# A gated mix of linear attention and a gMLP: token-major spatial product, one fused GELU ahead of all Exp, attention from unnormalised exponentials, DMA transposes

## The chip, the cores and the metric

The kernel runs on one core of one Trainium2 chip. The metric is device time in microseconds (us). Engines are named as in the profile: PE is the matrix engine (PEld its weight loads), DVE the vector engine, ACT the scalar (activation) engine, POOL the general engine, SP the engine whose queue issues most DMAs. A profiled span is some 2 us shorter than a timed run. Every ratio below is the mean time of one kernel's fast runs over the mean of the old kernel's fast runs of the same rounds on the same chip, with a 95% interval, so it is not quite the ratio of the medians that stand beside it.

## The reference

2048 tokens of width 512 go through two branches, which a sigmoid gate mixes. Branch A is linear attention with 32 heads of 16: the features are softmax(pq) and softmax(-pq). Branch B is a gMLP: GELU of an input product, half of it layer-normalised and multiplied over the token axis by a 2048x2048 matrix (the "spatial product"), times the other half, then an output product.

```python
pq = einsum('bhsd,hdf->bhsf', q, w_phi); pk = einsum('bhsd,hdf->bhsf', k, w_phi)
phi_q = concat([softmax(pq), softmax(-pq)]); phi_k = concat([softmax(pk), softmax(-pk)])
kv = einsum('bhsf,bhsd->bhfd', phi_k, v); z = einsum('bhsf->bhf', phi_k)
a = (phi_q @ kv / (phi_q @ z + 1e-06)) @ wo
zz = gelu(x @ w_in)                      # tanh form, 1376 features
z1, z2 = zz[..., :688], layernorm(zz[..., 688:])
b = (z1 * (w_sp @ z2 + b_sp[:, None])) @ w_out
out = g * a + (1 - g) * b                # g = sigmoid(x . gate_w)
```

## The kernel before

A first loop over 16 token tiles makes z2, the gate logit, K and V. GELU is built from five passes; Tanh and Exp are in use alternately (the trace has a single table load). `...` marks cuts.

```python
for tt in range(NT):
    ... # matmuls: z2_ps (128x689), v_ps, pk_ps
    nc.scalar.activation(out=xc[:, :], in_=z2_ps[:, 0:FH], func=AF.Copy)
    nc.vector.tensor_tensor(out=sq[:], in0=xc[:], in1=xc[:], op=ALU.mult)
    nc.vector.scalar_tensor_tensor(out=arg[:], in0=sq[:], scalar=INV_K, in1=xc[:], op0=ALU.add, op1=ALU.mult)
    nc.scalar.activation(out=th[:], in_=arg[:], func=AF.Tanh, scale=CK)
    nc.vector.scalar_tensor_tensor(out=z2all[:, tt, :], in0=th[:], scalar=1.0, in1=xc[:],
        op0=ALU.add, op1=ALU.mult, accum_out=s_z2[:, tt:tt + 1])
    nc.scalar.activation(out=junk[:], in_=z2all[:, tt, :], func=AF.Square, accum_out=s_sq[:, tt:tt + 1])
    ... # ek = exp(+-pk) on ACT; zk (reduce), rk (reciprocal), phik = ek * rk on DVE
```

The second half works feature-major in chunks of 512 tokens. z2 is the stationary operand of the spatial product (`lhsT` in the code; the other operand, `rhs`, is passed through it column by column, and these are the moving columns), so 688 features take six tiles of 128, the last with 48 useful rows but the full cost in moving columns. Attention normalises through PE: a block mask product sums the exponentials, and further products make denominators and spread their reciprocals.

```python
def gg_chunk(c, z1p, ft_list, uT, wspT):
    for ft in ft_list:                     # 6 feature tiles, the last 48 wide
        for st in range(NT):
            nc.tensor.matmul(gg_ps[0:m, :], lhsT=z2all[:, st, ft * P:ft * P + m], rhs=wspT[:, st, :], ...)
        ... # + bias row, * z1 (two DVE passes of 128x512)
def q_pre(c):
    for g in range(NDT):
        ... # e1, e2 = exp(+-pq)
        nc.tensor.matmul(s2p[:, :], lhsT=mask_bd[:, :], rhs=e2[:, :], ...)   # sums, spread
        nc.vector.tensor_tensor(out=phi1[:, :], in0=e1[:, :], in1=s2p[:, :], op=ALU.mult)
        ... # the same for phi2
    ... # den_ps: 8 products
def o_chunk(c, phi, rden):
    for g in range(NDT):
        nc.tensor.matmul(rbp[:, :], lhsT=selp[:, g, :], rhs=rden[:, :], ...)  # spread 1/den
        ... # nump: 2 products; ot = nump * rb
```

The softmax here doesn't subtract the row's maximum and nothing guards it: scores larger than these inputs give would overflow.

## Time and profile before

| | before |
|---|---|
| time, median (range) | 281.97 us (280.68 to 283.1) |
| profiled span | 279.6 us |
| PE, DVE, ACT busy | 246.8, 216.2, 148.4 us |
| moving columns on PE, counted in the source | about 548,500 |

The head of the page gives busy time per engine, and the span in 40 slices of 7 us, each digit a busy share in tenths (9 is 90% or more).

```profile
span 279.6 us, 3333 instructions
...
PE 246.8 (88%) x1213; PEld 112.6 (40%) x1236; DVE 216.2 (77%) x398; ACT 148.4 (53%) x263; POOL 6.7 (2%) x23
...
PE   0668799999888369999999999999999999999993
...
DVE  0067999999999999999989954589965489955442
```

DVE is at its top from the fifth slice to the twentieth, PE from the sixteenth to the last but one; before that PE falls to 3 tenths in one slice. The table of stages makes it firm. Its columns are the stretch and its length in us, busy us (and instructions) of PE, PEld, DVE, ACT and POOL, the share of its full clock that PE was granted, the DMA share and GB/s.

```profile
14.00:106.00 92.00, 75.27 (x434) 37.43 (x442) 86.62 (x176) 69.03 (x132) 0.00 (x0) 0.94 0.41 91
...
124.00:270.00 146.00, 145.06 (x644) 62.82 (x655) 109.34 (x175) 58.21 (x100) 0.00 (x0) 1.00 0.16 40
60.00:90.00 30.00, 26.88 (x148) 12.95 (x148) 30.00 (x56) 26.09 (x50) 0.00 (x0) 1.00 0.00 1
```

In the first loop (14 to 106 us) PE is idle for 92.00 - 75.27 = 16.7 us and DVE is 94% busy, from 60 to 90 us without a gap; in the second (124 to 270) PE has 145.06 of 146. So two different limits follow each other, with a stretch between (106 to 140 us, not shown) in which both engines are nearly full. The chain of waits says the same:

```profile
PE 57%; DVE 29%; ACT 4%; SPq 4%; DMA 3%; issue 2%; ACTq 0%
```

The passes of the built-up GELU in the list of groups (busy us, then mean ns of one, then idle time before them):

```profile
L214 DVE SCALAR_TENSOR_TENSOR z2all<-th,xc 128x688 bf16<-128x688 bf16 x16 | 14.0, 873 | 0.5 <-ACT th L213 0.5
L211 DVE SCALAR_TENSOR_TENSOR arg<-sq,xc 128x688 bf16<-128x688 bf16 x16 | 14.0, 873 | 0.1
...
L213 ACT ACTIVATE th<-arg 128x688 bf16<-128x688 bf16 x16 | 12.5, 780 | 7.6 <-DVE arg L211 7.4
L206 ACT ACTIVATE xc<-z_ps 128x688 bf16<-128x688 f32 x16 | 11.8, 735 | 15.6 <-PE z_ps L202 15.6
...
L209 DVE TENSOR_TENSOR sq<-xc 128x688 bf16<-128x688 bf16 x16 | 7.9, 495 | 0.0
```

### The profile page before, as it was taken

What the parts mean: (1) busy time and instruction counts of PE and PEld (TensorE: products, weight loads), DVE (VectorE), ACT (ScalarE), POOL (GpSimd) and SP (SyncE); (2) the same over time, 40 slices, a digit from 0 to 9 for tenths busy, and PEclk for the clock granted to TensorE, in tenths of its full rate; (3) what the DMA queues carried; (4) which work ended last, traced back from release to release, by engine and by line L of the source; (5) the groups of instructions that cost most, each with busy time, mean ns of one, the idle gap of its engine ahead of it and who ended that gap; (6) DMA issues with size and microseconds to landing.
All of it is one profiled execution on the core that took longest, in us unless ns stands there. A gap on an engine that the chain in (4) does not pass through costs nothing.

```text
span 279.6 us, 3333 instructions
## 1 busy us (share of the span) xinstructions
PE 246.8 (88%) x1213; PEld 112.6 (40%) x1236; DVE 216.2 (77%) x398; ACT 148.4 (53%) x263; POOL 6.7 (2%) x23
## 2 busy tenths in 40 slices
PE   0668799999888369999999999999999999999993
PEld 0234444444443137334434444444444444444441
DVE  0067999999999999999989954589965489955442
ACT  1154777897898649772448512158622156332033
POOL 9000000000000000000000000000000000000000
PEclk9998999999999879999999999999999999999999
DMA  6999997000000000000019110076010000010001
GB/s 167 218 233 232 221 263 248 4 0 0 0 2 0 0 0 4 0 0 2 1 28 272 40 38 0 1 175 146 19 38 0 2 0 0 19 60 0 0 19 56
DMA packets 51727, 17.53 MB, mean 63 GB/s; under 512 B 46800, under 2 KB 51584, under 8 KB 51712
## 3 DMA queue, kind: packets, MB, share of 16 engines
q1 hardware_dynamic: 51568, 16.81, 25.8%
q0 software_dynamic: 144, 0.52, 0.7%
q8 instruction: 9, 0.15, 0.2%
q14 instruction: 6, 0.05, 0.1%
HBM read 3.70 MB, written 2.10 MB: 21 GB/s over the span
## 4 chain that ended last, share of the span: by engine, by line
PE 57%; DVE 29%; ACT 4%; SPq 4%; DMA 3%; issue 2%; ACTq 0%
PE gg_ps L416 29%; PE z_ps L371 6%; PE b_ps L434 6%; DVE zk L228 5%; DVE phik_st L242 4%; PE a_ps L440 4%; DVE z2all L214 4%; DVE arg L211 3%; DMA wqkT<-in_A_wqkv_dram 3%; DVE phik_lv L236 3%; DVE rk L233 3%; PE den_ps L358 3%; SPq L114 2%; PE rbp L399 2%; DVE sq L209 1%
## 5 line engine op out<-in xcount | busy, mean ns | idle before, releaser
L416 PEld LDWEIGHTS <-z2all 128*128 128x128 bf16 (+1 forms) x384 | 37.4, 98 | 48.1 <-issue 5.2
L416 PE MATMUL gg_ps<-wsp_87,z2all 128*128 128x512 bf16 (+1 forms) x188 | 45.4, 379 | 0.2
L416 PE MATMUL gg_ps<-wsp_88,z2all 128*128 128x512 bf16 (+1 forms) x188 | 44.5, 379 | 0.2
L201 PE MATMUL z_ps<-w_in_g,xT 128*128 128x512 bf16 x62 | 22.7, 403 | 11.6 <-DMA w_in_g<-in_B_w_in_dram 9.1
L421 DVE TENSOR_TENSOR ggb<-gg_ps,brow 128x512 f32<-128x512 f32 (+1 forms) x24 | 16.4, 687 | 19.7 <-PE gg_ps L416 19.1
L401 ACT ACTIVATE rb<-rbp 128x512 bf16<-128x512 f32 x16 | 9.6, 597 | 40.6 <-PE rbp L399 40.6
L371 PE MATMUL z_ps<-xT,w_in_g 128*128 128x512 bf16 (+1 forms) x92 | 25.0, 398 | 1.5 <-DVE stat L207 1.1
L203 PE MATMUL v_ps<-wv_sb,xT 128*128 128x512 bf16 x61 | 20.6, 406 | 2.9 <-ACT vz_all L220 2.7
L206 ACT ACTIVATE xc<-z_ps 128x688 bf16<-128x688 f32 x16 | 11.8, 735 | 15.6 <-PE z_ps L202 15.6
L204 PE MATMUL pk_ps<-wk_p,xT 128*128 128x512 bf16 x63 | 17.7, 378 | 2.5 <-ACT ek L226 2.0
L228 DVE TENSOR_REDUCE zk<-ek 128x64 f32<-128x1024 bf16 x16 | 19.4, 1213 | 0.2 <-ACT ek L226 0.2
L260 PE MATMUL pq_ps<-xT,wq_p 128*128 128x512 bf16 x63 | 16.8, 379 | 0.4 <-ACT pqT_all L264 0.4
L452 ACT ACTIVATE ot_bf<-tmp,stat 128x512 bf16<-128x512 f32 x16 | 11.4, 720 | 10.3 <-DVE tmp L447 8.8
L213 ACT ACTIVATE th<-arg 128x688 bf16<-128x688 bf16 x16 | 12.5, 780 | 7.6 <-DVE arg L211 7.4
L202 PE MATMUL z_ps<-w_in_g,xT 128*128 128x177 bf16 x64 | 16.2, 254 | 0.1
L219 ACT ACTIVATE junk<-z2all 128x688 bf16<-128x688 bf16 x16 | 12.5, 780 | 6.6 <-DVE z2all L214 6.6
L447 DVE SCALAR_TENSOR_TENSOR tmp<-a_ps,stat,b_sb 128x512 f32<-128x512 f32 x16 | 11.3, 727 | 5.6 <-ACT b_sb L445 5.6
L445 ACT ACTIVATE b_sb<-b_ps 128x512 f32<-128x512 f32 x16 | 9.5, 591 | 10.7 <-PE b_ps L434 10.5
L371 PEld LDWEIGHTS <-w_in_g 128*128 128x128 bf16 (+1 forms) x96 | 9.4, 102 | 13.7 <-issue 5.3
L392 DVE RECIPROCAL rden<-den_ps 128x128 bf16<-128x128 f32 x16 | 14.5, 930 | 0.7 <-PE den_ps L358 0.7
L214 DVE SCALAR_TENSOR_TENSOR z2all<-th,xc 128x688 bf16<-128x688 bf16 x16 | 14.0, 873 | 0.5 <-ACT th L213 0.5
L211 DVE SCALAR_TENSOR_TENSOR arg<-sq,xc 128x688 bf16<-128x688 bf16 x16 | 14.0, 873 | 0.1
(486 smaller groups left out, 447.9 us busy)
## 6 DMA issues: line engine op xcount, KB each, us to landing
out_dram<-ot_bf SPq DMA_DIRECT2D x16, 128.0 KB, 1.7
w_in_g<-in_B_w_in_dram SPq DMA_DIRECT2D x2, 688.0 KB, 6.0
w_out_t<-in_B_w_out_dram SPq DMA_DIRECT2D x1, 640.0 KB, 6.4
brow<-in_B_b_sp_dram POOLq DMA_DIRECT2D x1, 512.0 KB, 5.6
wv_sb<-in_A_wqkv_dram SPq DMA_DIRECT2D x1, 512.0 KB, 7.6
wo_t<-in_A_wo_dram SPq DMA_DIRECT2D x1, 512.0 KB, 6.9
xT<-in_A_x_dram SPq DMA_TRANSPOSE x5, 4.9
w_out_t<-in_B_w_out_dram SPq DMA_DIRECT2D x1, 48.0 KB, 6.1
```

The lines of the kernel that those rows point to most:

```text
L201: nc.tensor.matmul(z2_ps[:, 0:CH], lhsT=lhsT, rhs=w_in_g[:, dt, FH:FH + CH], start=st_, stop=sp_)
L202: nc.tensor.matmul(z2_ps[:, CH:FH + 1], lhsT=lhsT, rhs=w_in_g[:, dt, FH + CH:F + 1], start=st_, stop=sp_)
L203: nc.tensor.matmul(v_ps[:, :], lhsT=lhsT, rhs=wv_sb[:, dt, :], start=st_, stop=sp_)
L204: nc.tensor.matmul(pk_ps[:, :], lhsT=lhsT, rhs=wk_p[:, dt, :], start=st_, stop=sp_)
L211: nc.vector.scalar_tensor_tensor(out=arg[:], in0=sq[:], scalar=INV_K, in1=xc[:], op0=ALU.add, op1=ALU.mult)
L214: nc.vector.scalar_tensor_tensor(out=z2all[:, tt, :], in0=th[:], scalar=1.0, in1=xc[:], op0=ALU.add, op1=ALU.mult, accum_out=s_z2[:, tt:tt ...
L228: nc.vector.tensor_reduce(out=zk[:, :], in_=ek[:].rearrange("p a (h e) -> p (a h) e", e=DH), axis=AX.X, op=ALU.add,)
L260: nc.tensor.matmul(pq_ps[:, :], lhsT=wq_p[:, dt, g * P:(g + 1) * P], rhs=xT[:, dt, c0:c0 + CH], start=(dt == 0), stop=(dt == NDT - 1),)
L371: nc.tensor.matmul(z1_ps[0:m, :], lhsT=w_in_g[:, dt, jt * P:jt * P + m], rhs=xT[:, dt, t0:t0 + CH], start=(dt == 0), stop=(dt == NDT - 1),)
L416: nc.tensor.matmul(gg_ps[0:m, :], lhsT=z2all[:, st, ft * P:ft * P + m], rhs=wspT[:, st, :], start=(st == 0), stop=(st == NT - 1),)
L421: nc.vector.tensor_tensor(out=ggb[0:m, :], in0=gg_ps[0:m, :], in1=brow[0:m, t0:t0 + CH], op=ALU.add)
L434: nc.tensor.matmul(b_ps[:, :], lhsT=uT[ft][:, t4 * P:(t4 + 1) * P], rhs=w_out_t[:, ft, :], start=(ft == 0), stop=(ft == NFT - 1),)
```

## The change

The intent is fewer PE columns and far less DVE work. (1) z2 becomes the moving operand of the spatial product (344 of 688 features at a time, no padding; the output has tokens on partitions, so the bias is a per-partition scalar and one DVE pass replaces two). (2) One fused GELU activation replaces the five passes, and the whole GELU stage is written ahead of everything with Exp, because the two need different ACT tables. (3) For queries the raw exponentials are multiplied by [kv | z | block mask] in one 144-column product; sums and denominators come out as columns, and the division is done on the 512 outputs per token. (4) What is now token-major (attention output, gated features) is brought to the output products by DMA transposes. (5) `w_sp` is loaded whole. The core of the diff, cut:

```diff
-        nc.scalar.activation(out=xc[:, :], in_=z2_ps[:, 0:FH], func=AF.Copy)
-        ... sq, arg, th, z2all (as above)
+    def z2_tile(tt):
+        zp = z_mm(tt, FH, FH + 1)
+        nc.scalar.activation(out=z2v, in_=zp[:, :, 0:HF], func=AF.Gelu_apprx_tanh)
+        ... # bn_stats, bn_aggr for the layer norm
+    for c in range(NCH):                   # all of z2 and z1 before the first Exp
+        for tt in ts: z2_tile(tt)
+        for tt in ts: z1_tile(tt)
+        z2_norm(ts)
 ...
+    def attn_tile(tt):
+        for a in range(2):
+            for g in range(NG):
+                nc.tensor.matmul(at[:, a, g, 0:AW], lhsT=eq[a][:, g, t0:t0 + P], rhs=kvz[:, a * 4 + g, :], ...)
+        ... # sd, t12, den, rden, r (small), m = at * r, o = m0 + m1
+        nc.sync.dma_start_transpose(out=oT[:, :, :], in_=o[:, :])
+    def gg_half(tt, j):
+        for st in range(NT):
+            nc.tensor.matmul(gp[:, :], lhsT=wspT[:, st, tt * P:(tt + 1) * P],
+                             rhs=z2all[:, st, j * HF:(j + 1) * HF], ...)
+        nc.vector.scalar_tensor_tensor(out=ucat[tt % NU][:, j * HF:(j + 1) * HF], in0=gp[:, :],
+            scalar=bT[:, tt:tt + 1], in1=z1all[:, tt, j * HF:(j + 1) * HF], op0=ALU.add, op1=ALU.mult)
+    def u_T(tt):
+        nc.sync.dma_start_transpose(out=uT[:, :, :], in_=ucat[tt % NU][:, :])
+    for tt in range(NT):
+        gg_half(tt, 0)
+        if tt >= 1: oTs[tt - 1] = attn_tile(tt - 1)
+        gg_half(tt, 1)
+        uTs[tt] = u_T(tt)
+        if tt >= 2: ba_tile(tt - 2, ...)   # 4 + 6 output products, one scaled copy, store
```

## The prediction

> **What bounds the kernel now.** The page shows a span of 279.6 us with PE busy 246.8 (88%), DVE 216.2 (77%), ACT 148.4 (53%). The table of stages shows three parts. To 9 us PE waits for input weights (one 9.1 us wait in the list of waits). From about 14 to 106 us DVE sets the pace: the tanh-GELU built from DVE and ACT passes (sq 495 ns, arg 873, z2all 873), zk 1213, rk 556, phik 556+827; in 60 to 90 us DVE is busy 30.0 of 30, PE 26.9. From 124 us to the end PE is full at clock 1.00 (29.9 of 30). The chain of waits agrees: PE 57%, DVE 29%.
>
> **Cost of PE work.** In the trace a 128x512 matmul starts every 215 ns, a 128x129 one every 57 ns, weight loads hidden: the N/2.4 + 2.5 ns of the Trainium skill, "TensorE: Matmul & The Clock Gate", section "Back-to-back issue gap". Counting moving columns from both sources: before 548,500 (229 us at full rate), after 484,000 (202 us; about 206 with the fixed cost). Saved: the padded sixth feature tile of spatial product and z1, and the ones-mask, denominator and broadcast products, partly offset by 144-column attention products.
>
> **What DVE and ACT lose.** One GELU activation replaces copy, sq, arg, tanh and the final product. From the 735 ns copy of 128x688 I estimate 0.74 us; "ScalarE: Activation LUTs" of the Trainium skill, section "Step-by-step: what each stage is for", says throughput does not depend on the function; no run here shows it yet. DVE estimates scaled from traced passes: bn_stats 0.45 us each, normalise 0.45.
>
> **Stage by stage (estimates).**
> - Start: first matmul at 8.5 us (w_in now split over ACT's queue).
> - GELU stage: 88,000 columns, 37.5 us on PE; ACT about 24 plus extra table loads (the order shows the gate's Exp placed between GELUs; 1.3 us each), DVE about 23. PE-bound with a cold clock at first: ends at 48.
> - Weight folding: eight 0.69 us casts in a row, partly covered by v and k products: 6 us, to 54.
> - K/V/Q stage: per tile PE 3.05, ACT 5 x 0.6 = 3.0, DVE 1.21+0.56+1.3 = 3.1 us, balanced; 50 us, to 104; draining the last tiles' DVE chain adds 3: 107.
> - Spatial/attention/output stage: per tile PE (32x344 + 8x144 + 10x512 columns) 7.3 us, DVE about 3.7; 117.6 us. The transposed attention output is needed about 7 us after its DVE chain allows issue, and two transposes are issued in order on SP. With the input transposes' 4.7 to 4.9 us landing and 1.3 us issue the margin is under 1 us, so I allow 5 us of PE stalls: 230.
> - Tail: DVE chain of the last tile, transpose, ten matmuls, store: 9 us, span about 239; times run about 2 us over the span.
>
> Predicted 240 us, 80% range 228 to 262. Chances: faster by over 2% 0.91, within 2% 0.03, slower 0.06.
>
> **What would show each step.** PE busy about 212 and over 88% of the span; DVE near 150, ACT near 100; gp matmuls every 146 ns; no stage with DVE above 90% except perhaps K/V/Q; PE waits on oT small; inputs (14 MB) landed by about 65 us.
>
> **What would make it wrong.** SBUF-to-SBUF transposes costing far more than input ones (issue of several us each): every output tile would wait, adding 16 times the excess. Next: the K/V/Q stage, where three balanced engines may wait for each other (+5 to 10 us); start-up DMA order; Pool's pow or DVE broadcast reads from PSUM slower than estimated.

## The result

The new kernel takes 237.0 us (236.57 to 238.69, 4 runs) against 281.33 us (280.3 to 283.1): ratio 0.8432, interval 0.8381 to 0.8482. The profiled span fell from 279.6 to 235.2 us. The page of the new kernel, the same lines as before (slices are now 5.9 us):

```profile
span 235.2 us, 3568 instructions
...
PE 212.9 (91%) x1412; PEld 127.9 (54%) x1412; DVE 149.0 (63%) x335; ACT 82.1 (35%) x133; POOL 9.9 (4%) x38
...
PE   0289999969999999995999999999999999999953
...
DVE  0035747677999999997177745577455775556750
```

PE busy fell by 33.9 us and PE's idle time by 10.5 us (from 32.8 to 22.3); together that is the 44.4 us of the span. The chain of waits is now

```profile
PE 62%; DVE 28%; DMA 6%; issue 2%; ACT 1%; SPq 1%; POOLq 0%; DVEq 0%; POOL 0%; ACTq 0%
```

Most of DVE's share in it is the K chain of the K/V/Q stage (phik 8%, zk 7%, rk 4%); e9 asks whether that chain sets the pace.

I cut the stages where the trace shows the last matmul of the GELU stage (54.5 us), the first K sum on DVE (60.15), and the first and last spatial matmul (109.4, 221.3):

```profile
12.87:54.50 41.63, 39.71 (x254) 25.20 (x254) 25.75 (x86) 25.64 (x35) 5.07 (x8) 1.00 1.19 236
54.50:60.15 5.65, 5.54 (x49) 3.40 (x49) 5.19 (x10) 4.02 (x6) 0.00 (x0) 1.00 1.30 284
60.15:109.40 49.25, 46.02 (x305) 24.66 (x304) 47.07 (x57) 40.13 (x77) 0.00 (x0) 1.00 0.08 25
109.40:221.30 111.90, 111.89 (x762) 70.90 (x763) 65.66 (x175) 8.94 (x13) 0.00 (x0) 0.98 0.28 59
221.30:235.20 13.90, 7.69 (x40) 3.09 (x37) 5.29 (x12) 2.06 (x3) 0.00 (x0) 1.00 0.25 61
```

The spatial stage has PE busy 111.89 of 111.90 us, so PE has no gap there; e3 tests whether its columns set the time. The groups that answer to those of before, and the spatial product:

```profile
L371 PE MATMUL gp<-z2all,wspT 128*128 128x344 bf16 x512 | 81.1, 313 | 0.8 <-DVE kvz L319 0.8
...
L184 DVE BATCH_NORM_STATS2 bn_83<-z2all 128x6 f32<-128x344 bf16 x32 | 14.9, 501 | 0.0
L181 ACT ACTIVATE z2all<-zp 128x688 bf16<-128x688 f32 x16 | 11.9, 744 | 15.2 <-PE zp L172 15.2
```

The fused GELU takes 744 ns for 128x688, as much as the plain copy of before (735). And the transposes that the prediction feared, from the list of DMA issues (count, then median us from issue to landing):

```profile
oT<-o SPq DMA_TRANSPOSE x16, 2.5
uT<-ucat_96 SPq DMA_TRANSPOSE x6, 2.8
```

Against the prediction, stage by stage (all in us of the span):

| | predicted | measured |
|---|---|---|
| matmuls run without gaps from | 8.5 | 12.9 (six at 5.3, then a wait) |
| GELU stage ends | 48 | 54.5 |
| weights folded | 54 | 60.2 |
| K/V/Q stage and its drain end | 107 | 109.4 |
| PE stalls in the spatial stage | 5 | about 0 |
| span | 239 | 235.2 |

### The profile page after: what moved, and what is told of

Read it like the earlier page. It is cut to its first block, busy times and chain, and to the rows that moved or that the text cites. A ratio compares the mean times of both kernels' runs of the same rounds, so it can differ in the third digit from the quotient of the medians.

```text
span 235.2 us, 3568 instructions
## 1 busy us (share of the span) xinstructions
PE 212.9 (91%) x1412; PEld 127.9 (54%) x1412; DVE 149.0 (63%) x335; ACT 82.1 (35%) x133; POOL 9.9 (4%) x38
## 4 chain that ended last, share of the span: by engine, by line
PE 62%; DVE 28%; DMA 6%; issue 2%; ACT 1%; SPq 1%; POOLq 0%; DVEq 0%; POOL 0%; ACTq 0%
PE gp L371 32%; PE zp L172 14%; DVE phik L273 8%; PE ba_ps L391 8%; DVE zk L266 7%; PE ba_ps L389 5%; DMA xT<-in_A_x_dram 5%; DVE rk L271 4%; PE at L335 3%; DVE bn_83 L184 1%; DVE wk_p L236 1%; DVE wq_p L236 1%; DMA oT<-o 1%; DVE m L356 1%; DVE z2all L201 1%
## 5 line engine op out<-in xcount | busy, mean ns | idle before, releaser
L371 PE MATMUL gp<-z2all,wspT 128*128 128x344 bf16 x512 | 81.1, 313 | 0.8 <-DVE kvz L319 0.8
L371 PEld LDWEIGHTS <-wspT 128*128 128x128 bf16 x512 | 50.1, 99 | 26.8 <-issue 0.9
L172 PE MATMUL zp<-w_in,xT 128*128 128x344 bf16 (+1 forms) x256 | 41.4, 324 | 10.8 <-DMA xT<-in_A_x_dram 10.6
L172 PEld LDWEIGHTS <-xT 128*128 128x128 bf16 x256 | 25.6, 101 | 28.0 <-DMA xT<-in_A_x_dram 11.2
L391 PE MATMUL ba_ps<-w_out_t,uT 128*128 128x512 bf16 x96 | 23.3, 379 | 0.0
L273 DVE TENSOR_TENSOR phik<-ek,rk 128x1024 bf16<-128x1024 bf16 x16 | 19.6, 1223 | 1.3
L356 DVE TENSOR_TENSOR m<-at,r 128x1024 f32<-128x1024 f32 x16 | 19.6, 1224 | 0.5
L389 PE MATMUL ba_ps<-wo_t,oT 128*128 128x512 bf16 x64 | 16.6, 380 | 2.6 <-DMA oT<-o 2.6
L376 DVE SCALAR_TENSOR_TENSOR ucat_96<-gp,bT,z1all 128x344 bf16<-128x344 f32 x12 | 6.9, 571 | 18.8 <-PE gp L371 18.8
L253 PE MATMUL k_ps<-wk_p,xT 128*128 128x512 bf16 x64 | 16.9, 378 | 0.0
L256 PE MATMUL v_ps<-wv_sb,xT 128*128 128x512 bf16 x64 | 16.7, 379 | 0.0
L376 DVE SCALAR_TENSOR_TENSOR ucat_97<-gp,bT,z1all 128x344 bf16<-128x344 f32 x10 | 5.7, 570 | 13.0 <-PE gp L371 13.0
L376 DVE SCALAR_TENSOR_TENSOR ucat_98<-gp,bT,z1all 128x344 bf16<-128x344 f32 x10 | 5.7, 570 | 11.9 <-PE gp L371 11.9
```

What stands on the lines that cost most here:

```text
L172: nc.tensor.matmul(zp[:, j, 0:n], lhsT=lhsT, rhs=w_in[:, dt, c0 + j * HF:c0 + j * HF + n], start=(dt == 0), stop=(dt == NDT - 1),)
L253: nc.tensor.matmul(k_ps[:, :], lhsT=xT[:, dt, t0:t0 + P], rhs=wk_p[:, dt, :], start=(dt == 0), stop=(dt == NDT - 1))
L256: nc.tensor.matmul(v_ps[:, :], lhsT=xT[:, dt, t0:t0 + P], rhs=wv_sb[:, dt, :], start=(dt == 0), stop=(dt == NDT - 1))
L273: nc.vector.tensor_tensor(out=phik[:, :].rearrange("p (h e) -> p h e", e=DH), in0=ek[:].rearrange("p a (h e) -> p (a h) e", e=DH), in1=rk[ ...
L356: nc.vector.tensor_tensor(out=m[:].rearrange("p a (g h d) -> p (a g) h d", g=NG, d=DH), in0=at[:, :, :, 0:P].rearrange("p a g (h d) -> p ( ...
L371: nc.tensor.matmul(gp[:, :], lhsT=wspT[:, st, tt * P:(tt + 1) * P], rhs=z2all[:, st, j * HF:(j + 1) * HF], start=(st == 0), stop=(st == NT ...
```

## The experiments

All runs gave the reference's result. Eleven kernels ran, in three jobs. Of the old kernel's runs in the first job one took 656.5 us and counts as slow; it is left out of the ratios. So is one execution each of e6, e7, e8 and e10 (240.27, 236.91, 237.65 and 232.51 us); the medians include them. The jobs ran on different chips, and a0, the new kernel unchanged, has the ratio 0.8468 where the main run had 0.8432: 1 us of doubt on any difference between jobs.

### e1: the fused GELU undone in the new kernel

```diff
-        nc.scalar.activation(out=z2v, in_=zp[:, :, 0:HF], func=AF.Gelu_apprx_tanh)
+        tanh_gelu(z2all[:, tt, :], zp)     # copy, sq, arg, tanh, product: the old passes (z1 likewise)
```

> The new kernel with one part undone: each fused GELU replaced by the old five passes (copy and tanh on ACT, square, add-multiply, add-multiply on DVE). My theory: the GELU stage stops being PE-bound and becomes DVE-bound. DVE per pair of tiles: 2 x (0.50+0.87+0.87) + 1.37 (statistics) + 0.45 (normalise) = 6.3 us against 2.3 us of PE, so 16 pairs take about 101 us in place of 41: time about 237+58 = 295 us, DVE at 90% or more in the stage. Only one table load is left in the whole program (Tanh and Exp come without a switch), which gives 2 to 3 us back. Rival (the gain is PE columns alone, GELU passes are hidden): under 247 us.

Measured: 292.22 us, ratio 1.0366 (1.0295 to 1.0437), slower than the old kernel. The last GELU-stage matmul starts at 103.5 us instead of about 54. In that stage DVE is busy for 82.26 of 90 us, and PE, often idle, is granted 0.79 of its clock:

```profile
14.00:104.00 90.00, 57.24 (x289) 31.58 (x289) 82.26 (x171) 43.23 (x58) 5.92 (x6) 0.79 0.63 138
```

So the GELU passes were not hidden: without the fused activation the rewrite loses 55 us and more than its whole gain.

### e5: the fused GELU alone, in the old kernel

```diff
-        ... xc, sq, arg, th, z2all (five passes)
+        nc.scalar.activation(out=z2all[:, tt, :], in_=z2_ps[:, 0:FH], func=AF.Gelu_apprx_tanh,
+                             accum_out=s_z2[:, tt:tt + 1])
```

(and the same for z1, with the constants that the five passes had put in; order and everything else kept)

> The old kernel with one part done alone: its five-pass GELU replaced by the fused GELU activation, everything else and its order kept. GELU and Exp then alternate, 53 table loads. My theory: the DVE pace of the first stage (5.7 us per tile) is only exchanged for an ACT pace (0.74+0.2+0.98+0.6+1.2+2.57 = 6.3 us per tile), so no gain: 275 to 300 us. Rival (the fused GELU by itself is the gain, whatever the order): the first stage falls to PE's 3.9 us per tile, about 252 us.

Measured: 298.39 us, ratio 1.0602 (1.0523 to 1.0682). The stretch from 60 to 90 us, which in the old kernel (shown above) had DVE at 30.00 and ACT at 26.09, now has

```profile
60.00:90.00 30.00, 20.37 (x107) 9.25 (x108) 15.68 (x25) 29.77 (x50) 0.00 (x0) 1.00 0.00 1
```

DVE's load is halved and ACT is full instead; PE does less in that stretch than before (20.37 against 26.88). The pace was exchanged, as expected. The fused GELU is worth nothing in the old order.

### e2: what the order is worth, measured by itself

In the new kernel, one GELU of a single column between the Exps of every K/V/Q tile:

```diff
+        nc.scalar.activation(out=jk[:, :], in_=k_ps[:, 0:1], func=AF.Gelu_apprx_tanh)
```

> The new kernel with one one-column GELU added between the Exps of every K/V/Q tile (its result is not used); 36 table loads in place of 4. My theory of why GELU goes ahead of all Exp: each added pair of loads takes at least 2 x 1.28 us of ACT, ACT per tile goes from 3.0 to at least 5.7 us against DVE 3.0 and PE 3.0, so the K/V/Q stage grows by 16 x 2.7 = 43 us or more: 280 us or more. Rival (table loads hide in ACT's idle time, ACT is only 35% busy): under 245 us.

Measured: 272.33 us, ratio 0.9665 (0.9608 to 0.9721). The direction is as expected and the rival is out, but the size is not: about 35 us, where I wrote 43 or more. ACT in order of time (start us, duration us):

```profile
80.26 0.60 ACT L259 ACTIVATE ek<-k_ps 128x512 bf16<-128x512 f32 x1
80.73 0.62 ACT L260 ACTIVATE ek<-k_ps 128x512 bf16<-128x512 f32 x1
81.37 1.28 ACT L262 ACT_TABLE_LOAD   x1
82.66 0.17 ACT L262 ACTIVATE jk<-k_ps 128x1 bf16<-128x1 f32 x1
82.73 0.59 ACT L264 ACTIVATE vz<-v_ps 128x512 bf16<-128x512 f32 x1
83.34 1.28 ACT L301 ACT_TABLE_LOAD   x1
84.63 1.08 ACT L301 ACTIVATE eq<-pq 128x512 bf16<-128x512 f32 x2
85.61 0.60 ACT L259 ACTIVATE ek<-k_ps 128x512 bf16<-128x512 f32 x1
```

A tile takes 85.61 - 80.26 = 5.35 us. The loads cost what I took, 1.28 us each. What I took too large is the rest: an Exp is recorded with 0.60 us, but the next one starts 0.47 to 0.48 us after it. So the five 128x512 passes need about 2.4 us of ACT per tile, not the 3.0 that I got by adding durations. That holds for the prediction as well, which called ACT balanced with PE and DVE in this stage.

### e3: is the spatial stage bound by PE columns?

```diff
-        gp = psC.tile([P, HF], FP32, name="gp", bufs=2)
+        gp = psC.tile([P, HF + 40], FP32, name="gp", bufs=2)   # 384 columns, 40 not used
```

> The new kernel with the spatial product's moving width 384 in place of 344 (40 columns computed and thrown away), which makes its column count that of the old orientation with its padded sixth tile (196,608). My theory: the stage is bound by PE columns, so 512 x 40 / 2.4 GHz = 8.5 us more: 245.5 us, the tile period going from 7.32 to 7.85 us. Rival (the stage waits for the DVE chain and the transposes, so PE has slack): under 239 us.

Measured: 246.74 us, ratio 0.8749 (0.8699 to 0.8799). Against the new kernel of the next job (ratio 0.8468) that is 0.0281 of 281 us = 7.9 us more (8.9 against the main run's 0.8432); the stage from first to last weight load grew from 111.6 us (109.4 to 221.0) to 120.9 (109.7 to 230.6), where 8.5 was expected. A tile takes 7.85 us in place of 7.32, which is 8.5 us over 16 tiles:

```profile
130.94 2.76 PE L371 MATMUL gp<-z2all,wspT 128*128 128x384 bf16 x16
...
138.79 2.76 PE L371 MATMUL gp<-z2all,wspT 128*128 128x384 bf16 x16
```

So here a column costs its time, and the padding of the old orientation, which had exactly this number of columns, was worth about 8 us (an estimate: it was not taken out of the old kernel).

### e4: every transpose issued twice

```diff
+        nc.sync.dma_start_transpose(out=xT[:, 2 + tt % 2, 0:D]..., in_=o[:, :])        # not read
         nc.sync.dma_start_transpose(out=oT[:, :, :], in_=o[:, :])
```

(the same for the gated features)

> The new kernel with every transpose of the spatial stage issued twice, the first time into a place that nobody reads. In the new kernel the attention transpose lands 2.2 us before PE needs it (landing 219.1 us of the span, use 221.3), and the sync queue is busy 3 of 7.3 us per tile. Doubling puts two more issues of 1.21 us ahead of it in place of one: margin about 1 us left. Theory (the transposes are hidden): the tile period stays at 7.32 us, only the tail grows by 1 to 2 us: 238.5 us, below 241. Rival (the transposes are already at the edge): the period grows by 1 us or more: 253 us or more.

Measured: 242.7 us, ratio 0.8633 (0.8585 to 0.8682): between the two expectations. The profiled run separates stage and tail. The spatial products run from 109.3 to 222.5 us, 113.2 us against 111.6, so the period stayed near 7.32 and the steady state hides even the double load but for 1.6 us: in the whole stage PE waits for a transpose twice, 1.14 us for the first one and 0.49 us near the end. From the last spatial weight load to the end it takes 17.2 us against 14.2: there is nothing left to hide the transposes, PE waits 2.94 and 0.60 us for the last two (2.1 and 0.5 in the new kernel), and after the longer wait its clock is down to 0.50 for some 2 us. The theory is right for the loop, and I underrated the tail. The rival of a stage at its edge is out.

### e9: the K/V/Q stage, which engine sets its pace?

```diff
         nc.vector.reciprocal(out=rk[:], in_=zk[:])
+        nc.vector.reciprocal(out=rj[:], in_=zk[:])      # not used
```

> The new kernel with the reciprocal of the K sums computed twice in every K/V/Q tile (0.55 us of DVE more per tile, not used). Theory from the trace (the DVE chain zk, rk, phik sets the 3.05 us period; DVE busy 50.3 of 53 us): the period becomes 3.6 us, 16 x 0.55 = 8.8 us more: 246 us. Rival (PE sets the period, DVE has slack): within 2 us of 237.

Measured: 240.79 us, ratio 0.8551 (0.8501 to 0.8601): 2.3 us more by the ratios (0.8551 against 0.8468; 3.3 us against the main run's 0.8432), not 8.8. My theory fell, and the rival as I had worded it (within 2 us of 237) is not met either. In the new kernel both engines look full in this stage:

```profile
80.00:90.00 10.00, 10.00 (x71) 5.49 (x69) 9.58 (x11) 8.81 (x17) 0.00 (x0) 1.00 0.01 2
```

Yet DVE could take most of 0.55 us more per tile. The run with the doubled reciprocal shows how, in DVE's lines in order of time (two sums, then the rest of the first tile and the start of the second):

```profile
83.21 2.33 DVE L266 TENSOR_REDUCE zk<-ek 128x64 f32<-128x1024 bf16 x2
85.46 0.54 DVE L271 RECIPROCAL rk<-zk 128x64 f32<-128x64 f32 x1
85.92 0.49 DVE L273 RECIPROCAL rj<-zk 128x64 f32<-128x64 f32 x1
86.33 1.16 DVE L275 TENSOR_TENSOR phik<-ek,rk 128x1024 bf16<-128x1024 bf16 x1
87.41 0.54 DVE L271 RECIPROCAL rk<-zk 128x64 f32<-128x64 f32 x1
```

The next sums start at 89.36 us, so two tiles take 6.15 us, and DVE has no gap. From start to start, a sum (zk) costs 1.12 us (two in 2.25), a reciprocal 0.41 to 0.46, and phik 1.08; the recorded durations (1.21, 0.55, 1.16) overlap. So the added reciprocal costs 0.41 us and the three original passes 1.12 + 0.46 + 1.08 = 2.66 us, which is 0.4 us less than the tile period of 3.05. PE can't go below that period at this spacing: 12 matmuls of 512 columns at 215.7 ns and 8 of 129 at 57 ns are 3.04 us, and from 80 to 90 us PE has no gap.

But the edit changed more than the amount of work. With it the scheduler put the sums of two tiles together; the new kernel keeps the passes of a tile in a row for most of the stage:

```profile
86.52 1.21 DVE L266 TENSOR_REDUCE zk<-ek 128x64 f32<-128x1024 bf16 x1
...
87.77 0.55 DVE L271 RECIPROCAL rk<-zk 128x64 f32<-128x64 f32 x1
...
88.42 1.23 DVE L273 TENSOR_TENSOR phik<-ek,rk 128x1024 bf16<-128x1024 bf16 x1
```

The next sum starts at 89.56 us. In this order the same three passes take 1.25 + 0.65 + 1.14 = 3.04 us from start to start, as long as PE's tile. Where the new kernel itself interleaves two tiles, a tile takes 2.7 us (reciprocals at 67.16, 69.83 and 72.54 us). So a DVE that reads 95.8% busy had 13% to spare once two tiles were interleaved; in the order that the new kernel mostly keeps, DVE and PE are level, and no run shows spare time there. What the run did lose (2.3 us between the first K sum and the first spatial matmul: 51.6 us against 49.3) fits a DVE that is now just saturated (3.07 us a tile) and the drain of its last tiles, where PE waits 3.9 us for phik against 2.4.

### a0, e6, e7, e8: three holes on the chain, one at a time

The trace after shows three holes of PE. The first is at the end of the GELU stage; ACT's lines and the PE line that ends the hole, in order of time:

```profile
48.11 1.28 ACT L312 ACT_TABLE_LOAD   x1
...
49.40 0.22 ACT L312 ACTIVATE g_el<-glog 128x16 f32<-128x16 f32 x1
...
49.63 1.28 ACT L189 ACT_TABLE_LOAD   x1
...
50.93 2.02 ACT L189 ACTIVATE z1all<-zp 128x688 bf16<-128x688 f32 x3
...
53.11 1.35 PE L172 MATMUL zp<-w_in,xT 128*128 128x344 bf16 x8
```

The scheduler put the gate's Exp before the last z1 GELUs. Two table loads stop ACT for 2.8 us, so PE's three tiles in PSUM (the memory that its products go to) wait to be read, and from 50.8 to 53.1 us PE has only three small products to do. e6 ties that Exp to the first K tile. Second, the second transpose of x is issued at 2.15 us and lands at 12.9, beside 1.4 MB of `w_in` on ACT's queue; e7 moves the half that is not yet needed behind it. Third, the last attention tile is one step late; e8 takes the lag away.

```diff
# e6
+        if tt == 0: glog2 = zk * 0 + glog          # then g_el = exp(glog2)
# e7
-    nc.scalar.dma_start(out=w_in[:, :, 0:FH], in_=w_in_v[:, :, 0:FH])
+    nc.sync.dma_start(out=w_in[:, :, 0:FH], in_=w_in_v[:, :, 0:FH])
# e8
-        if tt >= 1: oTs[tt - 1] = attn_tile(tt - 1)
+        oTs[tt] = attn_tile(tt)            # the extra call at the last step goes
```

> The new kernel unchanged, on the chip of the next three, as their base: 237 us.

> The new kernel with the gate's Exp made to depend on the first K tile (a zero times its sum is added to the gate logits), so that it can't be scheduled among the GELUs; table loads 4 to 2. The profile shows ACT losing 2.8 us there and PE idle about 2 us at 51 to 53 us of the span, then waiting for wphi. Theory: that hole is on the chain, 2 to 3 us gained: 234.5 us. Rival (hidden under the DVE casts of the weight folding that follow): within 0.7 us of the unchanged kernel.

> The new kernel with the 704 KB load of the z1 half of w_in moved from ACT's queue to the sync queue, behind the transposes of the first 512 tokens of x. The profile shows the second x transpose issued at 2.2 us but landing at 12.9 us, while the w_in halves of ACT's queue move beside it. Theory: the sharing of the DMA engines delays it; without, it lands at about 8.5 us and the time falls by 3 to 4 us: 233.5 us. Rival (the transpose itself is slow, or z1's weights are then late): within 1 us of the unchanged kernel or slower.

> The new kernel with the attention tile done in the same step as its spatial tile, not one step later. Its output is then transposed a step earlier, so PE need not wait for the last two transposes (2.6 us of waits in the list). Theory: the tail shortens by 2 to 3 us, the rest is unchanged: 234.5 us. Rival (attention at the start of the stage waits for the K/V sums and gives it back): within 0.7 us.

| | median us | ratio to the old kernel (95%) | against a0, us (ratio difference x 281) |
|---|---|---|---|
| a0, unchanged | 237.44 | 0.8468 (0.8435 to 0.8501) | |
| e6 | 235.29 | 0.8368 (0.8339 to 0.8396) | -2.8 |
| e7 | 235.08 | 0.8357 (0.8320 to 0.8395) | -3.1 |
| e8 | 236.11 | 0.8384 (0.8349 to 0.8420) | -2.4 |

None of the three intervals overlaps that of a0, so each rival (within 0.7 or 1 us) is out. PE's mean granted clock differs between executions of one kernel, though, and that is a rival too. At like clock e6 gains 1.7 us (two executions against four of a0 at 0.993: 235.4 against 237.1 us), e7 3.3 (0.992 to 0.993) and e8 2.9 (0.978), so the gains stand; e6's other two ran at 1.000, and whether its edit or chance gave them that clock is open. The traces show the gains where they should be: the last weight load of the GELU stage starts at 51.6 us (e6) and 51.9 us (e7) instead of 53.8 in a0, and after the last spatial weight load e8 needs 11.3 us instead of 14.1. In e7 the x tile is there at 9.7 us instead of 12.9, so its 3 us are partly lost again before the stage ends.

One thing disturbs such small comparisons. The two profiles of the unchanged kernel differ by 2 us, and the difference starts at this very hole. The same stretch in a0, and then in the first profile:

```profile
54.00:56.00 2.00, 1.99 (x12) 1.22 (x12) 1.12 (x3) 0.74 (x1) 0.00 (x0) 0.55 1.11 225
56.00:58.00 2.00, 1.78 (x12) 1.09 (x12) 1.15 (x2) 0.03 (x1) 0.00 (x0) 0.60 1.27 290
...
54.00:56.00 2.00, 1.89 (x17) 1.00 (x15) 1.04 (x3) 0.74 (x1) 0.00 (x0) 1.00 1.15 258
56.00:58.00 2.00, 2.00 (x22) 1.34 (x21) 2.00 (x4) 1.14 (x2) 0.00 (x0) 1.00 1.28 290
```

In a0 the clock drops to 0.55 and 0.60 for about 4 us after the hole; in the first profile it stayed at 1.00 through it. That agrees with the Trainium skill, "TensorE: Matmul & The Clock Gate", section "Part 1: The HAM clock gate", which has the clock set by a free-running activity window, so that the same kernel can fall on either side.

A fourth hole was not tried. At the end of the K/V/Q stage PE waits 2.4 us for the last phik and 0.8 us for kvz, and then its clock is down to 0.63 (109 to 111 us) and 0.51 (111 to 113): the first 48 spatial matmuls take 8.84 us in the first profile. In e7's profile, where the clock stayed up, they take 7.16 us.

### e10: all three together

> The new kernel with the three single edits together: the gate's Exp kept out of the GELU stage, the z1 weights loaded behind the first x transposes on the sync queue, attention without the one-tile lag. If the three gains (by the ratios of the last job 2.8, 3.1 and 2.4 us) stand on separate parts of the chain they add: 229 us. If the start only moves the same hole or the stages hide each other: 232 us or more.

Measured: 230.39 us (228.88 to 232.51), ratio 0.8173 (0.8128 to 0.8219). The three differences of the last table sum to 0.0295, and 0.8468 - 0.0295 = 0.8173: they add, within an interval of 1.3 us either way (that the last digit agrees is luck). This version beats both kernels; it is 3.5% faster than the new one by these ratios (3.1% against 0.8432). Its page:

```profile
span 229.2 us, 3568 instructions
...
PE 212.9 (93%) x1412; PEld 128.3 (56%) x1412; DVE 148.2 (65%) x336; ACT 79.4 (35%) x131; POOL 9.8 (4%) x38
```

PE is busy as long as before; only idle time went.

## Why the prediction was right

240 us was predicted, 237.0 measured, inside the range. The mechanism was right in its main steps. That the total came so close is partly luck: of the span's stages the prediction was 6.2 us early at the end of the folding (54 against 60.15), gave 3.8 us too much to the K/V/Q stage with its drain (53 against 49.25) and 6.2 us too much to the rest (132 against 125.8). Point by point:

- **Columns.** Predicted PE busy 212, measured 212.9; the count itself gave 206, and the prediction doesn't say where the other 6 us come from. The count of 548,500 to 484,000 moving columns is 26.9 us at full rate. e3 confirms the price of a column in the spatial stage (20,480 columns: 7.9 to 8.9 us in the times, 8.5 by the tile period, 9.3 from first to last weight load, against 8.5); the other two thirds of the saved columns were counted and not tested.
- **The DVE pace.** DVE busy was predicted at 150 and is 149.0. The old first loop left PE idle for 16.7 us. That and the 26.9 us of columns are 43.6 us, near the 44.4 that the span lost, but this is no check: PE's whole idle time fell by 10.5 us only, since new waits came, and its busy time by 33.9. The parts don't act alone either. e1 and e5 show that: the rewrite without the fused GELU is at 1.04 of the old time, the fused GELU without the rewrite at 1.06, both together at 0.84.
- **GELU ahead of Exp.** The price of a swap was right (1.28 us a load); e2 puts the value of the order at 35 us for 32 more loads. The fused GELU at 744 ns confirms the estimate of 0.74 us from the copy and what "ScalarE: Activation LUTs", section "Step-by-step: what each stage is for", says of throughput, that it does not depend on the function.
- **Mis-sized, start and GELU stage:** I gave 8.5 us and 48 us; measured 12.9 and 54.5. I left out that `w_in` on the other queue delays the x transpose (e7), and I counted the gate's table loads as ACT time only, where they open a hole in PE (e6).
- **Mis-sized, the transposes:** I took the 4.7 to 4.9 us landing of the input transposes for those inside SBUF. They land in 2.5 and 2.8 us, the 5 us of stalls did not come, and e4 shows that the loop has room for twice as many. That made up for part of the late start.
- **Mis-sized without effect on the time:** "three balanced engines" in the K/V/Q stage. By spacing instead of durations PE needs 3.04 us and ACT 2.4 per tile (e2), so ACT was not in balance; DVE needs 2.66 interleaved (e9) but 3.04 in the order that the new kernel mostly keeps, so for DVE and PE the word was right, though reached by adding durations. ACT busy was predicted near 100 and is 82.1. The period came out right because PE's own estimate, 3.05, was right.

Left open: how the 7 us by which PE's busy time fell beyond the columns' 26.9 us divides between clock (0.981 on average before, 0.993 after) and single matmuls that end without a successor; no run took these apart. Nor does any run take out the attention products of (3) or the whole load of `w_sp` of (5) alone.

## What to carry to other kernels

Count moving columns and multiply by the spacing that the trace shows; here that gave 206 us of the 212.9 that PE was busy, and for one stage's tile 3.04 of 3.05. For DVE and ACT take the spacing from start to start in a saturated stretch, not the sum of durations, before you call an engine full, and look at the order: passes that wait for each other took 3.04 us in a row and 2.7 us with another tile's pass between them. Two parts of a rewrite can each lose alone and win together: a fused activation whose table differs from its neighbour's is worth its price only once all uses of one table are gathered, and then one stray activation that the scheduler moves between them costs twice a load and the hole behind it.

## What the Trainium skill lacked or had wrong

- "ScalarE: Activation LUTs", section "What ACT_TABLE_LOAD costs", gives 2.66 us for every switch (load and drain). Here a switch took the 1.28 us load and little else: in e2 the next activation starts 0.01 us after the load ends, and the load starts 0.64 us after an Exp that is otherwise followed in 0.47; over the tile (5.35 us less five passes at 0.48 and 0.07 for the added GELU) it is about 1.4 us a switch.
- "Perfetto Trace Analysis", section "Identifying the Most-Contended Engine", calls DVE's occupancy a fair measure of how close it is to its limit. In the K/V/Q stage DVE read 9.58 of 10 us busy, and with two tiles interleaved (e9) it took 0.41 us more per tile at a period of 3.07 us in place of 3.05. The same page's section "Optimizing Scalar/DVE Operations" has the reason (recorded latency counts about twice the access overhead of an instruction, because the half that acknowledges the write overlaps the next instruction), and the spacing of 1.12 us for a sum recorded with 1.21 agrees in kind.
- "DMA: Bandwidth & Descriptors" has no time from issue to landing on trn2 for a transpose from SBUF to SBUF. Here: 1.21 us of issue, landing 2.5 us after the issue for 128x512 bf16 and 2.8 us for 128x768.
- No page that I found times batch-norm statistics or POOL's power: here 501 ns were recorded for 344 bf16 columns on DVE, and 1.04 us for 128x4 fp32 on POOL.
